# The cost figures of a list schedule: DMA transposes and overlapping VectorE operations (local attention beside a gated MLP, one core)

## The chip, the cores and the metric

The kernel runs on one core of a Trainium2 chip. The metric is the time of one execution on the device, in microseconds (us). The core has a matrix engine (PE, TensorE), a vector engine (DVE, VectorE), an activation engine (ACT, ScalarE), GpSimd (POOL) and a fifth one, SP (SyncE), which here does nothing but issue DMAs. Each engine takes its instructions strictly in the order in which they were written to its queue; engines wait for each other through semaphores.

## The reference

```python
x = A_x                                    # 1 x 2048 x 512, bf16
xn = layernorm(x)
# A: local, dilated attention: 32 heads of 16, window of 8 positions, dilation 2
q, k, v = split(xn @ wqkv)
logits[s, w] = q[s] . k[s - 2 w] * 0.25    # masked where s - 2 w < 0
o[s] = sum_w softmax(logits)[s, w] * v[s - 2 w]
A = o @ wo
# B: gMLP with a spatial gate, Fh = 896
z = gelu(xn @ w_in);  z1 = z[:, :896];  z2 = layernorm(z[:, 896:])
g = w_sp @ z2 + b_sp[:, None]              # w_sp is 2048 x 2048
B = (z1 * g) @ w_out
out = x + A + B
```

## The kernel before

The 2048 positions are cut into 16 blocks of 128 (index b) and 4 groups of 512 (index j or tc). The program is first written down as a list of some 900 tasks, each with an engine, an estimated duration (`est`), what it reads and writes, and a priority (a small number is urgent). `Plan.schedule` (L122) then plays the program through with these estimates and so fixes the order of every engine's queue; `Plan.emit` writes the queues and the semaphore waits. The estimates have no other effect: nothing of the planned times is in the program but the order.

The tasks, with the names used below:

- `ln_block(b)`, L569: x is loaded (`ldx`); DVE takes its statistics (`bnst` L574, `bnag` L576) and adds epsilon (`vpe` L597); POOL raises it to the power -0.5 (`rstd`, L600); DVE normalises (`norm`, L602); SP transposes the block by DMA (`xTd`, L606, 128 KB). The first four blocks are also centred (L582), transposed on PE (`xTr`, L589) and copied by ACT (L594), so that PE can start sooner. Warm-up matmuls (`warm`, L559) fill PE before that.
- `v_block` (L630 and on) makes v and stores it to DRAM (`Vw`, on POOL's queue, L638). `z2_block` (L728) makes the second half of z, with gelu and sums on ACT (L734, L739). `z2_wave(j)` works out its normalisation for four blocks at a time: four small DVE operations (L745 to L752), a power on POOL (`zr`, L755, estimate 1.9 us), four DVE normalisations (`zn`, L758).
- `qk_pair` (L647) makes q and k; `prods(j)` multiplies q with the eight shifted copies of k on DVE (`prod`, L668) and adds up four groups (`padd`, L673); PE reduces over the head dimension (`red`, L681, 32 small matmuls, priority 1); `softmax(j)` follows on DVE and ACT (L691 to L717).
- `z1_group` (L772) makes the first half of z, priority 200 and up.
- `ld_wT(tc)` transposes w_sp by DMA from DRAM (L829, 16 pieces of 512 KB, priority 6 and up). `g_group` (L856) multiplies with it, priority 300 and up; ACT copies the result (L864), DVE adds the bias and multiplies with z1 (`gb` L867, `u` L870).
- `pv_block(b)`: SP loads the eight shifted copies of v (`ldVs`, L879, 1 MB, priority 5); DVE multiplies with the attention weights and adds up (`pv` L884, L887, L890); SP transposes the result by DMA (`OTd`, L893, 128 KB, priority 2).
- `out_block(b)`: the residual is loaded (`ldxr`, L902, priority 4); PE multiplies OT with wo (L912) and the gated z1 with w_out (L921), priority 250 plus b (400 plus b for the last four blocks); DVE adds the residual (`fin`, L927); SP stores (`st`, L932, priority 3).

The schedule works as follows. For each engine it takes the candidate tasks whose dependencies are all planned, finds the earliest time at which one of them could start, and of all that could start within `tol` of this takes the one with the smallest priority. Of the engines' picks the earliest is planned. A compute task holds its engine for `est`. A task that depends on it is ready at its end plus a `hop`: 220 ns behind PE, 25 ns behind the same engine, 60 ns behind another, 100 ns behind a DMA. A DMA holds its queue for `issue` (480 ns on SP and ACT, 600 ns on POOL); 400 ns later it joins one line in which all transfers follow one another, at `dma_bw` bytes per ns, or `xbar_bw` for a transpose (265 at most in the first 7 us); it has landed 1300 ns after its turn ends. The estimate of a DVE operation of two tensors is c_tt(n) = 152 + n / 1.92 ns, so 2285 ns for 4096 elements; of bn_stats it is 685 ns.

Of the kernel before, what the change touches and what calls it, by code (L numbers as in the profile page):

```python
# [36 lines left out]
class Plan:  # L37
# [81 lines left out]
        return t  # L119


    def schedule(self, dma_bw=340.0, xbar_bw=190.0, dma_lat=1300.0, dma_pre=400.0, issue=None, tol=40.0):  # L122
        issue = issue or {"sp": 480.0, "act": 480.0, "pool": 600.0}
        for t in self.tasks:
            t.nwait = len(t.deps) + len(t.odeps)
            t.ready = 0.0
        for t in self.tasks:
            for d in t.deps | t.odeps:
                d.outs.append(t)
        cand = {e: [t for t in self.tasks if t.eng == e and t.nwait == 0] for e in ENGS}  # L130
        free = {e: 800.0 for e in ENGS}
        free["pool"] = 500.0
        free["sp"] = 790.0
        order = {e: [] for e in ENGS}
        dma_free = 0.0
        tbl = None
        slots = [dict(prev=None, avail=0.0) for _ in range(8)]
        left = len(self.tasks)

        def hop(d, t):  # L140
            if d in t.odeps:
                return 0.0
            if d.dma is not None:
                return 100.0
            if d.eng == "pe":
                return 220.0
            return 25.0 if d.eng == t.eng else 60.0

        def place(b, now):
            best = None  # L150
            if b.n == 2:
                opts = [(i, i + 1) for i in (0, 2, 4, 6)]
            else:
                opts = [(i,) for i in range(8)]
            for o in opts:
                if any(slots[i]["prev"] is not None and slots[i]["prev"].left > 0 for i in o):
                    continue
                av = max(slots[i]["avail"] for i in o)
                mate = 0.0
                if b.n == 1:  # L160
                    m = slots[o[0] ^ 1]
                    mate = 0.0 if (m["prev"] is not None and m["prev"].left > 0) else 1.0
                key = (max(av, now) + 300.0 * mate, av)
                if best is None or key < best[0]:
                    best = (key, o, av)
            return best

        while left:
            pick = None
            for e in ENGS:  # L170
                sc = []
                for t in cand[e]:
                    r = max(t.ready, free[e])
                    for b in t.banks:
                        if b.base is None:
                            p = place(b, r)
                            if p is None:
                                r = None
                                break
                            r = max(r, p[2])  # L180
                    if r is not None:
                        sc.append((r, t))
                if not sc:
                    continue
                st = min(r for r, _ in sc)
                near = [(t.prio, t.idx, r, t) for r, t in sc if r <= st + tol]
                near.sort(key=lambda x: x[:2])
                r, t = near[0][2], near[0][3]
                if e == "act" and t.tbl is not None and tbl is not None and t.tbl != tbl:
                    stay = [x for x in near if x[3].tbl in (None, tbl)]  # L190
                    if stay and stay[0][0] < t.prio + t.late:
                        r, t = stay[0][2], stay[0][3]
                if pick is None or r < pick[0]:
                    pick = (r, e, t)
            if pick is None:
                print("free", free, "slots", [(s_["prev"].name, s_["prev"].left) if s_["prev"] else None for s_ in slots])
                for e in ENGS:
                    print(e, [(t.name, t.ready, [(b.name, b.base) for b in t.banks]) for t in cand[e]][:12])
                raise RuntimeError("scheduler stuck")
            r, e, t = pick  # L200
            if t.drop and r > 9000.0:
                t.start = t.end = t.eng_end = r
                for b in t.banks:
                    b.left -= 1
                    if b.left == 0:
                        for sl in slots:
                            if sl["prev"] is b:
                                sl["avail"] = r
                cand[e].remove(t)
                left -= 1  # L210
                for o in t.outs:
                    o.ready = max(o.ready, r)
                    o.nwait -= 1
                    if o.nwait == 0:
                        cand[o.eng].append(o)
                continue
            for b in t.banks:
                if b.base is None:
                    _, o, av = place(b, max(t.ready, free[e]))
                    b.base = o[0]  # L220
                    prevs = {id(slots[i]["prev"]): slots[i]["prev"] for i in o if slots[i]["prev"] is not None}
                    for pb in prevs.values():
                        for u in pb.users:
                            if u.eng == e == "pe":
                                t.odeps.add(u)
                            elif u is not t:
                                t.deps.add(u)
                    for i in o:
                        slots[i]["prev"] = b
            t.start = r  # L230
            if t.dma is not None:
                iss = issue[e]
                t.eng_end = r + iss
                bw = xbar_bw if t.dma.get("xbar") else dma_bw
                xs = max(r + iss + dma_pre, dma_free)
                xe = xs + t.dma["nbytes"] / (bw if xs > 7000.0 else min(bw, 265.0))
                dma_free = xe
                t.end = xe + dma_lat
            else:
                dur = t.est  # L240
                if t.tbl is not None:
                    if tbl is not None and t.tbl != tbl:
                        dur += 1300.0
                    tbl = t.tbl
                t.eng_end = t.end = r + dur
            free[e] = t.eng_end
            for b in t.banks:
                b.left -= 1
                if b.left == 0:
                    av = max(u.end + (220.0 if u.eng == "pe" else 60.0) for u in b.users)  # L250
                    for s in slots:
                        if s["prev"] is b:
                            s["avail"] = av
            cand[e].remove(t)
            order[e].append(t)
            left -= 1
            for o in t.outs:
                o.ready = max(o.ready, t.eng_end if t in o.odeps else t.end + hop(t, o))
                o.nwait -= 1
                if o.nwait == 0:  # L260
                    cand[o.eng].append(o)
        self.order = order
        self.makespan = max(t.end for t in self.tasks)
# [736 lines left out]
```

## Time and profile before

| | |
|---|---|
| median of three runs | 241.48 us (241.38 to 242.04) |
| the profiled execution | 242.56 us |
| its span, first to last instruction | 240.0 us |
| granted PE clock, mean | 0.998 of full speed |
| PE busy | 233.5 us |
| DVE busy, instructions | 214.8 us, 271 |
| ACT, POOL busy | 98.3 us, 29.4 us |
| DMA transposes, SP | 16 (L606), 16 (L829), 16 (L893) |

The profile is one execution, recorded by the hardware. A row of a timeline gives the start in us, the duration in us, engine, line, operation, the tile written and the tile read, and the number of like instructions merged; in square brackets stands for how long the engine sat idle ahead of it and which instruction ended that. PE's matmuls overlap, so their durations are longer than their distance; the distance between starts is what counts. The times of a DMA on SP's queue are those of the issuing instruction; its landing is told separately. In the chain of waits "issue" is time in which an engine waited for nothing that the profile shows.

### The profile page before, as it was taken

What the parts mean: (1) busy time and instruction counts of PE and PEld (TensorE: products, weight loads), DVE (VectorE), ACT (ScalarE), POOL (GpSimd) and SP (SyncE); (2) the same over time, 40 slices, a digit from 0 to 9 for tenths busy, and PEclk for the clock granted to TensorE, in tenths of its full rate; (3) what the DMA queues carried; (4) which work ended last, traced back from release to release, by engine and by line L of the source; (5) the groups of instructions that cost most, each with busy time, mean ns of one, the idle gap of its engine ahead of it and who ended that gap; (6) DMA issues with size and microseconds to landing.
All of it is one profiled execution on the core that took longest, in us unless ns stands there. A gap on an engine that the chain in (4) does not pass through costs nothing.

```text
span 240.0 us, 3184 instructions
## 1 busy us (share of the span) xinstructions
PE 233.5 (97%) x1210; PEld 112.6 (47%) x1232; DVE 214.8 (90%) x271; ACT 98.3 (41%) x147; POOL 29.4 (12%) x56
## 2 busy tenths in 40 slices
PE   7999999999999999999999999999999999999994
PEld 4555555555444444544454444444444444444443
DVE  4868999898999999999999989989989999999932
ACT  2599869888898885721112111001010100101200
POOL 2566510406224100000000000000000000000000
PEclk9999999999999999999999999999999999999999
DMA  6997969999527210013079999999999978941121
GB/s 199 363 284 118 244 134 175 181 193 216 160 94 262 83 35 9 0 41 136 0 249 299 210 220 257 182 248 319 349 344 347 278 249 261 267 64 22 22 66 46
DMA packets 79966, 43.35 MB, mean 181 GB/s; under 512 B 52288, under 2 KB 79312, under 8 KB 79952
## 3 DMA queue, kind: packets, MB, share of 16 engines
q1 hardware_dynamic: 78720, 40.72, 67.1%
q0 software_dynamic: 800, 2.11, 2.4%
q10 hardware_dynamic: 432, 0.31, 0.4%
q8 instruction: 10, 0.16, 0.3%
q14 instruction: 4, 0.03, 0.1%
HBM read 26.35 MB, written 4.21 MB: 127 GB/s over the span
## 4 chain that ended last, share of the span: by engine, by line
PE 70%; DVE 19%; POOL 5%; ACT 3%; issue 1%; DVEq 0%; ACTq 0%
PE ps L856 40%; PE ps L921 10%; PE ps L772 10%; PE ps L912 6%; DVE arena L673 6%; DVE arena L668 6%; POOL fpool L755 3%; PE ps L559 2%; DVE arena L758 2%; POOL fpool L600 2%; ACT arena L734 2%; DVE arena L602 1%; PE ps L681 1%; DVE fpool L574 1%; PE ps L630 1%
## 5 line engine op out<-in xcount | busy, mean ns | idle before, releaser
L856 PE MATMUL ps<-arena 128*128 128x512 bf16 x437 | 98.2, 379 | 0.6
L856 PEld LDWEIGHTS ps<-arena 128*128 128x128 bf16 x448 | 43.7, 98 | 52.4
L864 ACT ACTIVATE arena<-ps 128x1024 bf16<-128x1024 f32 (+1 forms) x16 | 14.7, 917 | 103.8 <-PE ps L856 99.7
L668 DVE TENSOR_TENSOR arena<-arena 128x4096 bf16<-128x4096 bf16 x16 | 36.5, 2286 | 0.1
L884 DVE TENSOR_TENSOR arena<-arena 128x4096 bf16<-128x4096 bf16 x16 | 36.5, 2284 | 0.0
L887 DVE TENSOR_TENSOR arena<-arena 128x2048 bf16<-128x2048 bf16 (+1 forms) x32 | 30.5, 955 | 0.6
L647 PE MATMUL ps<-arena 128*128 128x512 bf16 x124 | 28.7, 379 | 0.2
L673 DVE TENSOR_TENSOR arena<-arena 128x4096 bf16<-128x4096 bf16 x12 | 27.5, 2291 | 0.3
L921 PE MATMUL ps<-arena 128*128 128x512 bf16 (+2 forms) x117 | 26.9, 366 | 0.1
L728 PE MATMUL ps<-arena 128*128 128x448 bf16 x128 | 26.0, 352 | 0.0
L772 PE MATMUL ps<-arena 128*128 128x512 bf16 x110 | 24.4, 379 | 0.1
L647 PEld LDWEIGHTS ps<-arena 128*128 128x128 bf16 x128 | 14.5, 113 | 13.0
L656 ACT ACTIVATE arena<-ps 128x1024 bf16<-128x1024 f32 x16 | 16.2, 1018 | 4.4 <-PE ps L647 3.2
L728 PEld LDWEIGHTS ps<-arena 128*128 128x128 bf16 x128 | 12.4, 98 | 11.7
L927 DVE TENSOR_TENSOR arena<-ps,arena 128x512 bf16<-128x512 f32 (+2 forms) x17 | 11.1, 656 | 7.5 <-PE ps L921 7.1
L921 PEld LDWEIGHTS ps<-arena 128*128 128x128 bf16 x119 | 11.5, 98 | 12.7
L772 PEld LDWEIGHTS ps<-arena 128*128 128x128 bf16 x112 | 10.8, 97 | 13.2 <-issue 0.4
L912 PE MATMUL ps<-arena 128*128 128x512 bf16 (+2 forms) x68 | 16.6, 366 | 0.0
L778 ACT ACTIVATE arena<-ps 128x1024 bf16<-128x1024 f32 (+1 forms) x16 | 14.0, 920 | 5.4 <-PE ps L772 5.3
L630 PE MATMUL ps<-arena 128*128 128x512 bf16 x61 | 15.9, 386 | 0.2
L739 ACT ACTIVATE arena<-arena 128x896 bf16<-128x896 bf16 x16 | 15.2, 949 | 0.1
L574 DVE BATCH_NORM_STATS2 fpool<-arena 128x6 f32<-128x512 bf16 x16 | 11.0, 687 | 2.4 <-DMA arena<-in_A_x_dram 2.4
(60 smaller groups left out, 178.0 us busy)
## 6 DMA issues: line engine op xcount, KB each, us to landing
arena<-vscr SPq DMA_DIRECT2D x16, 1024.0 KB, 6.2
arena<-in_A_x_dram SPq DMA_DIRECT2D x30, 128.0 KB, 4.0
vscr<-arena POOLq DMA_DIRECT2D x16, 128.0 KB, 2.8
out_dram<-arena SPq DMA_DIRECT2D x15, 128.0 KB, 4.2
arena<-in_A_wqkv_dram SPq DMA_DIRECT2D x2, 512.0 KB, 6.5
arena<-in_B_w_in_dram SPq DMA_DIRECT2D x2, 448.0 KB, 5.9
arena<-in_B_w_in_dram SPq DMA_DIRECT2D x1, 896.0 KB, 6.6
arena<-in_B_w_out_dram SPq DMA_DIRECT2D x1, 896.0 KB, 5.4
```

The source lines that it names most:

```text
L630: last = t.matmul(P(bk, 512), xTv(b, dc), AC(off["wv"] + 512 * dc, [[1, 512]]), start=(dc == 0), stop=(dc == 3))
L647: last = t.matmul(P(bk, 512, 512 * which), AC(off["wqk"] + 2048 * which + 512 * dc + c, [[4, 128]]), AC(off["xnT"] + dc * S + 512 * j, [[1 ...
L656: T("act", lambda a: a.activation(AC(qo, [[ko - qo, 2], [1, 512]]), P(bk, 1024).rearrange("p (t n) -> p t n", t=2), ACTF.Copy, scale=0.5), ...
L668: T("dve", (lambda pbv, qb, kb: lambda v: v.tensor_tensor(pbv, qb, kb, ALU.mult))(pbv, qb, kb), reads=rd, writes=[("pb", s_)], est=c_tt(40 ...
L673: T("dve", (lambda av, bv: lambda v: v.tensor_tensor(av, av, bv, ALU.add))(av, bv), reads=[("pb", 1)], writes=[("pb", acc)], est=c_tt(4096 ...
L728: last = t.matmul(P(bk, 448, 512 * hf), xTv(b, dc), AC(off["w_in2"] + 896 * dc + 448 * hf, [[1, 448]]), start=(dc == 0), stop=(dc == 3))
L772: last = t.matmul(P(bk, 512, 512 * i), AC(off["w_in1"] + 896 * dc + 128 * fc, [[1, 128]]), AC(off["xnT"] + dc * S + 512 * j, [[1, 512]]), ...
L856: last = t.matmul(P(bk, 512, 512 * i), AC(off["z2"] + FH * sh + 128 * fc, [[1, 128]]), AC(off["wT%d" % r_] + sh * 512, [[1, 512]]), start= ...
L884: T("dve", lambda v: v.tensor_tensor(tv, tv, av, ALU.mult), reads=[("attn", b)], writes=[("Vs", sv)], est=c_tt(4096), name="pv%d" % b, pri ...
L887: T("dve", (lambda n: lambda v: v.tensor_tensor(A("Vs", n, 4096 * sv), A("Vs", n, 4096 * sv), A("Vs", n, 4096 * sv + n), ALU.add))(n), wri ...
L912: last = t.matmul(P(bk, cn), AC(off["OT"] + 512 * tb + 128 * cc, [[1, 128]]), AC(off["wo"] + 512 * cc + c0, [[1, cn]]), start=(cc == 0), s ...
L921: last = t.matmul(P(bk, cn), AC(off["z1T"] + fc * S + 128 * tb, [[1, 128]]), AC(off["w_out"] + 512 * fc + c0, [[1, cn]]), start=False, sto ...
```

## The change

The change touches `Plan.schedule` alone. Five figures of the game are different:

```diff
-    def schedule(self, dma_bw=340.0, xbar_bw=190.0, ...
+    def schedule(self, dma_bw=340.0, xbar_bw=500.0, ...
...
-            return 25.0 if d.eng == t.eng else 60.0
+            if d.eng == t.eng == "dve":
+                return 100.0
+            return 25.0 if d.eng == t.eng else (135.0 if d.eng == "dve" else 60.0)
...
-                near = [(t.prio, t.idx, r, t) for r, t in sc if r <= st + tol]
+                near = [(t.prio, t.idx, r, t) for r, t in sc if r <= st + (110.0 if e == "dve" else tol)]
...
                 iss = issue[e]
+                if t.dma.get("xbar"):
+                    iss = 1300.0 if t.dma["nbytes"] <= 131072 else 3400.0
...
-                dur = t.est
+                dur = t.est - (75.0 if e == "dve" else 0.0)
```

A DMA transpose holds its queue for 1300 ns (128 KB) or 3400 ns (512 KB) where it held it for 480, and moves at 500 bytes per ns where it moved at 190. A DVE operation holds DVE for 75 ns less; its result is ready for DVE 100 ns and for another engine 135 ns after that, where it was 25 and 60. On DVE a task may be preferred that starts up to 110 ns after the earliest candidate, where it was 40. The tasks, their instructions, their tiles and their data are the same; a PSUM bank is given to a task in the order of the plan, so the bank of a tile can differ.

More of the change, by code (lines that the diff above doesn't have):

```diff
@@ L119, in add, with schedule @@
         return t
-    def schedule(self, dma_bw=340.0, xbar_bw=190.0, dma_lat=1300.0, dma_pre=400.0, issue=None, tol=40.0):
+    def schedule(self, dma_bw=340.0, xbar_bw=500.0, dma_lat=1300.0, dma_pre=400.0, issue=None, tol=40.0):
         issue = issue or {"sp": 480.0, "act": 480.0, "pool": 600.0}
```

## The prediction

> **What bounds the kernel now.** I read the page's busy table first, then its slices, then the waits of each engine, then the timelines of PE, DVE, POOL and SP.
>
> ```profile
> PE 233.5 (97%) x1210; PEld 112.6 (47%) x1232; DVE 214.8 (90%) x271; ACT 98.3 (41%) x147; POOL 29.4 (12%) x56
> ...
> PE   7999999999999999999999999999999999999994
> ...
> DVE  4868999898999999999999989989989999999932
> ```
>
> PE is full from the second slice to the last but one, DVE nearly so. Busy PE is only modelled, so I counted its work. From the timeline of PE the first useful matmul (L589) starts at 5.07 us; the last of L921 ends, and releases the last DVE add, at about 236.57: 231.5 us. In the chain of waits the g matmuls run like this:
>
> ```profile
> 101.11 10.74 PE ps L856 x49
> 111.85 0.05 issue
> 111.90 10.74 PE ps L856 x49
> 122.64 0.05 issue
> ```
>
> From 101.11 to 124.37 lie 108 of them (six groups of 16 and three quarters of the seventh): 0.215 us each, its 0.05 us pauses included. The others by their own rows, those 108 included: 917 matmuls of 512 columns x 0.215 = 197.2; 128 of 448 columns x 0.189 (32 in 6.06 us from 32.44 to 38.50) = 24.2; 128 small ones of L681 x 0.0247 (0.79 us for 32) = 3.2; 16 of L589 x 0.055 = 0.9; the last, split block about 2.4. Sum 227.9. So PE wastes 231.5 - 227.9 = 3.6 us at most between its first and last useful matmul. Before it lie 5.07 us (x arrives, DVE normalises), behind it 3.4 us to the span's end (last add, last store). **No order of the same operations can win more than that 3.6 us**, and most of it is the start: nine warm-up matmuls after 5.07 (0.8 us) and gaps of the first blocks. The later waits are these, the first two from the timeline of PE, the rest the whole list of PE's waits:
>
> ```profile
> 51.32 0.95 PE L681 MATMUL ps<-arena 128*128 128x32 bf16 x32 [0.46 <-DVE arena L673]
> 75.97 0.97 PE L681 MATMUL ps<-arena 128*128 128x32 bf16 x32 [0.16 <-DVE arena L673]
> ...
> PE ps L559 <- DVE arena L515: 1.3, 1, 1.3
> PE ps L681 <- DVE arena L673: 0.6, 2, 0.5
> ```
>
> Behind the warm-up (L559) PE waits 0.62 us in the whole kernel, both times for the last sum of a product group (L673, tasks padd0_3 and padd1_3) ahead of a reduction (L681, red0, red1).
>
> **The change part by part.** No operation is added or removed; the costs with which the list is made change, so each engine's fixed order may change, and the chip waits wherever that order asks for something that isn't there.
>
> *Transposes on SP.* The list gave every transpose 0.48 us of SP; now 1.3 (128 KB) or 3.4 (512 KB). The trace, by the views of the three lines:
>
> ```profile
> L606 SPq DMA_TRANSPOSE arena<-arena x16: 1200/1265/2436, 7.8 to 34.7; - x16
> ...
> L829 SPq DMA_TRANSPOSE arena<-in_B_w_sp_dram x16: 1716/2392/7242, 36.0 to 153.9; - x16
> ...
> L893 SPq DMA_TRANSPOSE arena<-arena x16: 1191/1202/1280, 144.2 to 227.5; - x16
> ```
>
> (min/median/max ns). 1.3 is right; 3.4 is 1.0 over the median, but six of the big ones from 125.24 took 18.95 us, 3.16 each. With the bandwidth now 500, a small one lands in the plan 1.3 + 0.4 + 0.26 + 1.3 = 3.26 us after issue starts (before 0.48 + 0.4 + 0.69 + 1.3 = 2.87); measured medians are 4.1 (L606) and 3.5 (L893). SP will thus seldom be planned too early. What this can move is the place of OTd (priority 2), stores (3), residual loads (4), Vs loads (5) and weight transposes (6 and up) among each other from 124 us on: when SP is planned busy, several are ready at once and priority decides. Gain on PE's path: none to take, since PE never waits there. Cover: from SP's rows and the 3.5 us, OT landed some 2.3 us ahead of its first matmul (L912) for block 0, 3.1 for block 5, 1.4 for block 9, about 0 for block 10, 3.0 for block 15. While that lasts the cost is 0.
>
> *DVE's overlap.* An instruction now occupies DVE 0.075 us less; one that needs its result still waits 0.1 (DVE) or 0.135 (others). For a dependent one nothing changes (bnst: 685 + 25 = 610 + 100); an independent one comes 0.075 earlier. The timeline of DVE shows this to be right:
>
> ```profile
> 71.30 2.29 DVE L668 TENSOR_TENSOR arena<-arena 128x4096 bf16<-128x4096 bf16 x1
> 73.62 2.29 DVE L673 TENSOR_TENSOR arena<-arena 128x4096 bf16<-128x4096 bf16 x1
> 75.83 2.28 DVE L668 TENSOR_TENSOR arena<-arena 128x4096 bf16<-128x4096 bf16 x1
> ```
>
> 2.32 us to the sum that needs the product, 2.21 to the next, independent product. The Trainium skill speaks against it: "VectorE: DVE Perf Modes", section "The DRAIN you can't avoid", says the next operation doesn't start until the pipe is empty, though it points to exceptions. By that rule the new list would hold DVE 271 x 0.075 = 20.3 us too fast and the kernel would end far later; by the rows it loses nothing, and the measurement decides.
>
> What it does: up to 271 x 0.075 = 20.3 us of planned DVE time go (the bound, were all independent). That allowance was false per instruction, but it paid for things the list still counts too short, so DVE reached its joins with PE not much late. Slack of the sum against the reduction that needs it, from both timelines: red0 -0.46, red1 -0.16, red2 100.09 - 99.17 = +0.9, red3 124.21 - 122.85 = +1.4 us. Since red has priority 1, the list puts it on PE at the instant its sum is planned to be ready; a sum late on the chip holds up the PE queue behind it, g, z1 and V included.
>
> *What is still counted too short.* The pow on POOL (L755), estimate 1.9 us:
>
> ```profile
> 44.16 3.00 POOL L755 TENSOR_TENSOR fpool<-fpool 128x4 f32<-128x4 f32 x1 [13.26 <-DVE fpool L752]
> ...
> 56.88 3.00 POOL L755 TENSOR_TENSOR fpool<-fpool 128x4 f32<-128x4 f32 x1 [1.39 <-DVE fpool L752]
> ...
> 79.89 1.04 POOL L755 TENSOR_TENSOR fpool<-fpool 128x4 f32<-128x4 f32 x1 [1.96 <-DVE fpool L752]
> ```
>
> Beside a 2.28 us product it takes 3.0, beside L696 1.04. Twice DVE then sits 0.91 and 0.93 us (L758) on a sum's path. The list sees none of it: 0.9 late at red0, 1.8 by red1. A Vs load is planned 0.48 + 0.4 + 3.08 + 1.3 = 5.3 us and measured 6.2.
>
> *DVE's window of choice* grows from 40 to 110 ns: a more urgent task may be awaited up to 0.11 us. At most some tens of such choices, about half a microsecond of DVE per ten, in a stage where DVE had 2.2 us of idle time for rstd (L602 behind L600) that the new list sees and may fill with the next bn_stats. I take 0 for the end: neither reaches PE while the reds set it.
>
> *Sum for PE:* lower bound -0.62 (both waits go) less perhaps 0.6 of the start; upper bound +1.8 - 0.62 = +1.2 at the reds, plus 0.9 if Vs loads come late with no slack left. I take one late pow at its full price, +0.9, less the 0.62 that PE waits there already: **+0.3 us**. Only one, since the second wave may come to lie beside a shorter operation, as the last one did. The profiled execution took 242.56 us with a span of 240.0 (2.56 around it); span about 240.3, 242.9 profiled. The runs shown have a median of 241.48, 1.08 under the profiled one, so **241.8**.
>
> **Rivals.**
>
> *Both pow waits turn into PE waits* (slower). For: reds are placed with no slack; red0 and red1 have already waited. Against: 0.6 us of it is already paid, and products may now start earlier by the filled rstd waits. It decides once the sum is planned over 0.62 us ahead of what the chip does. Price +1.2 to +1.5: **242.8**.
>
> *The out blocks lose their lead* (slower). Priority 250 puts them before g as soon as OT is planned to land. Their measured lead, 0 to 3.9 us, shrinks; a Vs load 0.9 late holds pv, OTd, then PE; a late add holds the store on SP (L932 sat there up to 1.87 us) and with it the next OTd. 0.9 + 1.6 = +2.5: **244.0**. Against: transposes are now planned at their true queue time.
>
> *Fewer waits* (faster). The 0.62 goes and 0.3 to 0.6 of the first 12 us: -0.9: **240.6**. For: the costs come nearer to the rows. Against: little is there to win, and the start follows x, bn_stats, centring, transpose and copy, whose latencies are unchanged.
>
> *The order hardly changes:* 241.5, inside the forecast.
>
> **How the numbers follow.** A measurement can tell about 0.3%, 0.72 us. Within it 0.41 (forecast and unchanged order); slower 0.38 (reds 0.27, out blocks 0.11); faster 0.21. Point 241.8. The range takes in the faster case and both waits at full price, and cuts half of the out-block case: 240.4 to 243.5. Both signs hold much, so the likeliest case's own range: 241.0 to 242.2.
>
> **What would show it.** Right: PE's waits still name L681 behind L673, 0.5 to 1.5 us in sum, and PE 97% busy. First rival: over 1.5 us there. Second: waits of L912 for a transpose or for L879. Faster: no wait of L681 and a first L647 matmul before 17.12. I am wrong if the pow's row stays at 1.0 everywhere, if DVE waits for Vs loads, or if ACT, 41% busy, shows up as a releaser of PE.

## The result and the profile after

The changed kernel takes **257.27 us** (median of 6 runs, 255.32 to 257.87); the kernel before, run beside it, 241.79 us (241.38 to 242.78). The ratio is 1.062, 95% interval 1.058 to 1.067: slower by 15.5 us, where the prediction had 241.8 us and a range of 240.4 to 243.5. The profiled execution took 257.87 us with a span of 255.4 at a mean granted clock of 0.993.

The diff adds four lines ahead of the tasks, so every line of the kernel before stands 4 further down: `red` is L685, `padd` L677, `z1` L776, `z1g` on ACT L782, `Ve` (ACT's copy of v) L639, its store `Vw` L642, `zr` L759, `rstd` L604, `OTd` L897, the weight transposes L833, the first matmul of an out block L916. In the experiments two more lines can be added (L916 becomes L918).

The page's busy row of PE, its slices and the granted clock by slices:

```profile
PE 236.4 (93%) x1210; PEld 112.5 (44%) x1231; DVE 215.2 (84%) x271; ACT 101.5 (40%) x149; POOL 31.9 (12%) x56
...
PE   8999999799989499999999878697899999999995
...
PEclk9999999999999979999999999999999999999999
```

The work is the same; PE now has holes: one "4" in slice 14 (83 to 89 us), shallower ones between slices 23 (140 us) and 29, and a clock of "7" in slice 15, behind the deepest hole. Smaller dips in slices 8 and 12 (45 to 51 and 70 to 77 us) are two reductions. The waits of PE say what the holes are (sum in us, number of times, longest):

```profile
PE ps L916 <- DMA arena<-arena: 7.9, 7, 2.0
PE ps L776 <- ACT arena L782: 3.8, 1, 3.8
PE ps L685 <- DVE arena L677: 1.4, 1, 1.4
...
PE ps L685 <- ACT arena L639: 0.8, 1, 0.8
```

Seven times an out block stood at the head of PE's queue before its OT had landed; once z1 waited for a PSUM bank that ACT empties; two reds waited. With the 0.2 us of z1 that the list puts down to issue this is 14.1 us behind the warm-up, against 0.62 before: 13.5 more. The rest is in the timeline of PE:

```profile
88.23 1.84 PE L776 MATMUL ps<-arena 128*128 128x512 bf16 x6 [3.75 <-ACT arena L782]
90.29 12.76 PE L776 MATMUL ps<-arena 128*128 128x512 bf16 x52 [0.22 <-issue]
...
143.68 1.04 PE L916 MATMUL ps<-arena 128*128 128x512 bf16 x4 [1.06 <-DMA arena<-arena]
...
165.05 1.04 PE L916 MATMUL ps<-arena 128*128 128x512 bf16 x4 [2.00 <-DMA arena<-arena]
```

From 88.23 to red2 at 102.88 the 60 or so z1 matmuls take 0.244 us each and not 0.215: the granted clock is 0.62 from 88.3 to 92 us and 0.92 to 96, 0.38 x 3.7 + 0.08 x 4 = 1.7 us lost. A third term comes from how a wait is counted: from the modelled end of the matmul ahead, 0.379 us after its start, where PE would have started the next one after 0.215. So each wait costs 0.16 us more than its row says; there are ten waits against two, 1.3 us more. 13.5 + 1.7 + 1.3 = 16.5; PE's last matmul ends 16.2 us later than before, and the stretch behind it is 0.8 us shorter. So the loss is PE waiting, and being slow behind one wait. The first out block now stands at 143.68 in PE's queue; before it came at 150.04, 3.3 us after its OT had landed.

The cause of the out blocks' waits is in the timeline of SP:

```profile
141.09 1.27 SPq L897 DMA_TRANSPOSE arena<-arena  x1
142.41 0.58 SPq L883 DMA_DIRECT2D arena<-vscr  x1
143.09 4.64 SPq L833 DMA_TRANSPOSE arena<-in_B_w_sp_dram  x1
147.77 1.27 SPq L897 DMA_TRANSPOSE arena<-arena  x1
```

and the same of the kernel before:

```profile
145.54 0.58 SPq L879 DMA_DIRECT2D arena<-vscr  x1
146.17 4.68 SPq L829 DMA_TRANSPOSE arena<-in_B_w_sp_dram  x1
150.90 1.26 SPq L893 DMA_TRANSPOSE arena<-arena  x1
```

A weight transpose behind one load of Vs holds SP for 4.6 us, in both. Before, six of them had gone ahead of OT0 and only two stood between OTs; now four do (4.64, 4.45, 4.59, 5.24 us). Each is planned at 3.4, so SP falls behind by 1.24 + 1.05 + 1.19 + 1.84 = 5.3 us over four blocks, and the four out blocks after the first wait 1.41 + 0.81 + 2.00 + 1.23 = 5.5.

That the kernel before had a lead to spare lies in its plan, the times by which `Plan.schedule` makes the order (they follow from the program; no trace shows them). There OT0 is issued at 140.3 us and lands at 150.7, 10.5 us later, because six weight transposes at 190 bytes per ns stand ahead of it in the one line of transfers; OT1 to OT3 get 13.2, 11.4 and 9.8 us. On the chip these four took 2.5, 4.1, 2.5 and 5.1 us from issue to landing. The queue was booked too cheaply (OT0 was issued at 144.2), the transfer far too dearly, and the second error covered the first. At 500 bytes per ns the line is empty: the plan of the changed kernel gives each of them 3.3 us. The chip takes 2.5 to 3.3, so this figure is right, and nothing is left to cover SP's late issues. No run separates the bandwidth from the queue time.

### The profile page after: what moved, and what is told of

The parts are those of the page before. It is cut to its first block, busy times and chain, and to the rows that moved or that the text cites. A ratio compares the mean times of both kernels' runs of the same rounds, so it can differ in the third digit from the quotient of the medians.

```text
span 255.4 us, 3185 instructions
## 1 busy us (share of the span) xinstructions
PE 236.4 (93%) x1210; PEld 112.5 (44%) x1231; DVE 215.2 (84%) x271; ACT 101.5 (40%) x149; POOL 31.9 (12%) x56
## 4 chain that ended last, share of the span: by engine, by line
PE 40%; DVE 35%; DMA 11%; POOL 6%; ACT 4%; issue 4%; DVEq 0%; ACTq 0%
PE ps L860 17%; DVE arena L672 9%; PE ps L925 8%; DMA arena<-arena 7%; PE ps L776 6%; DVE arena L677 5%; PE ps L916 5%; DMA vscr<-arena 4%; DVE arena L891 3%; DVE arena L888 2%; POOL fpool L759 2%; POOL fpool L604 2%; PE ps L563 2%; DVE fpool L578 1%; DVE arena L700 1%
## 5 line engine op out<-in xcount | busy, mean ns | idle before, releaser
L860 PE MATMUL ps<-arena 128*128 128x512 bf16 x437 | 98.6, 379 | 0.6
L776 PE MATMUL ps<-arena 128*128 128x512 bf16 x109 | 26.0, 395 | 4.1 <-ACT arena L782 3.8
L651 PE MATMUL ps<-arena 128*128 128x512 bf16 x125 | 28.6, 379 | 0.2
L677 DVE TENSOR_TENSOR arena<-arena 128x4096 bf16<-128x4096 bf16 x12 | 27.5, 2289 | 0.3
L916 PE MATMUL ps<-arena 128*128 128x512 bf16 (+2 forms) x68 | 16.7, 368 | 7.9 <-DMA arena<-arena 7.9
L776 PEld LDWEIGHTS ps<-arena 128*128 128x128 bf16 x112 | 11.2, 101 | 18.3 <-ACT arena L782 4.5
L871 DVE TENSOR_TENSOR arena<-arena 128x1024 bf16<-128x1024 bf16 (+1 forms) x16 | 9.9, 618 | 9.1 <-ACT arena L868 9.0
L782 ACT ACTIVATE arena<-ps 128x1024 bf16<-128x1024 f32 (+1 forms) x16 | 14.0, 917 | 7.0 <-PE ps L776 7.0
L634 PE MATMUL ps<-arena 128*128 128x512 bf16 x61 | 15.7, 387 | 0.2
```

The source lines that it names most:

```text
L634: last = t.matmul(P(bk, 512), xTv(b, dc), AC(off["wv"] + 512 * dc, [[1, 512]]), start=(dc == 0), stop=(dc == 3))
L651: last = t.matmul(P(bk, 512, 512 * which), AC(off["wqk"] + 2048 * which + 512 * dc + c, [[4, 128]]), AC(off["xnT"] + dc * S + 512 * j, [[1 ...
L677: T("dve", (lambda av, bv: lambda v: v.tensor_tensor(av, av, bv, ALU.add))(av, bv), reads=[("pb", 1)], writes=[("pb", acc)], est=c_tt(4096 ...
L776: last = t.matmul(P(bk, 512, 512 * i), AC(off["w_in1"] + 896 * dc + 128 * fc, [[1, 128]]), AC(off["xnT"] + dc * S + 512 * j, [[1, 512]]), ...
L860: last = t.matmul(P(bk, 512, 512 * i), AC(off["z2"] + FH * sh + 128 * fc, [[1, 128]]), AC(off["wT%d" % r_] + sh * 512, [[1, 512]]), start= ...
L916: last = t.matmul(P(bk, cn), AC(off["OT"] + 512 * tb + 128 * cc, [[1, 128]]), AC(off["wo"] + 512 * cc + c0, [[1, cn]]), start=(cc == 0), s ...
```

## The experiments

All runs stand beside runs of the kernel before on the same chip; ratios are to those. "Waits" are PE's, behind the warm-up.

**Each half alone.** e1 is the changed kernel with the old figures of the transposes (190 bytes per ns, 480 ns of queue); e2 is the kernel before with the new ones only.

```diff
 e2, on the kernel before
-    def schedule(self, dma_bw=340.0, xbar_bw=190.0, ...
+    def schedule(self, dma_bw=340.0, xbar_bw=500.0, ...
+                if t.dma.get("xbar"):
+                    iss = 1300.0 if t.dma["nbytes"] <= 131072 else 3400.0
```

> The changed kernel with the DMA transposes counted as in the kernel before (0.48 us of SP, 190 bytes per ns); only the VectorE figures are new. Theory (the lost allowance on VectorE takes the lead from PE's joins): this half carries the loss, PE waits again at the reductions, at z1 and at the out blocks, 253 to 258 us. Rival (the queue time of the transposes reorders SP and carries the loss): 241 to 243 us.

> The kernel before with the DMA transposes counted at 1.3 and 3.4 us of SP and 500 bytes per ns; VectorE as before. Theory: VectorE's allowance still hides what is counted too short, PE keeps its lead, 241 to 243 us, waits of PE under 2 us in sum. Rival (the SP figures carry the loss): 250 us or more, with PE waits for the transposes of the attention result.

e1: 246.39 us, ratio 1.020 (1.017 to 1.023). No out block waits (OT keeps its lead; in this plan it again lands 11 to 13 us after its issue for the first four blocks), the reds wait 4.2 us. e2: 249.06 us, 1.031 (1.027 to 1.034). The reds wait 0.2; the list of waits:

```profile
PE ps L914 <- DMA arena<-arena: 5.5, 3, 3.8
```

Behind the 3.80 us one the clock is 0.50 for 5.1 us. Neither expectation held: both halves cost, by different waits: the VectorE figures through the reds, the queue figures through the out blocks. They don't add up exactly (4.7 + 7.4 against 15.5), since every plan is another order.

**The out blocks.** e6 leaves the changed kernel's order alone and makes the last four weight transposes small; e3 tells the planner that OT lands 3 us later; e10 rearranges SP by hand; e8 gives the planner SP times near the measured ones; e9 gives it a large lead at both places.

```diff
 e6
+                nb_ = 1 if tc == 3 else NB      # destination and source cut to nb_ * 128 columns
 e3, in hop
-                return 100.0
+                return 3100.0 if d.name.startswith("OTd") else 100.0
 e10, on the finished order
+        put("sp", ["ldVs2", "ldVs3"], "OTd0")
+        for i_ in range(4):
+            put("sp", ["wT3_%d" % i_], "ldVs%d" % (4 + i_))
 e8
-                    iss = 1300.0 if t.dma["nbytes"] <= 131072 else 3400.0
+                    iss = 1300.0 if t.dma["nbytes"] <= 131072 else 2300.0 + 2500.0 * nvs   # Vs loads since the last big one
 e9, in hop
+            if t.name.startswith("red"):
+                return 2600.0
-                return 100.0
+                return 8100.0 if d.name.startswith("OTd") else 100.0
```

(`put` moves the named tasks ahead of another in one engine's order; e8 also books `zr` at 3.0 us.)

> The changed kernel, all orders the same, but the last four weight transposes on SP move one block of 128 columns instead of 16 (the rest of that quarter of the weights is left out). Theory S (the out blocks wait because SP sits 4.5 to 5.2 us at each weight transpose that stands behind a Vs load and ahead of a transpose of the attention result): the 7.9 us of PE waits for those transposes fall under 1.5 us, 247 to 251 us. Theory L (PE, VectorE and SP hold each other up in a loop, or the out blocks simply stand too early): 5 us or more of the waits stay, 253 to 257 us.

> The changed kernel, but the plan holds a landed transpose of the attention result ready for PE 3 us later, so that the out blocks stand some 2.6 us further back in PE's queue. Theory L (a loop: PE late, so the add late, so SP and the next transpose late): the 7.9 us of waits go to under 1 us, 249 to 251 us. Theory S (SP's own queue runs late, 4.6 us instead of 3.4 for each weight transpose, whatever PE does): the lateness of 6 to 8 us stays and 3 us of it is covered, 4 to 5 us of waits stay, 253.5 to 255.5 us.

> The changed kernel, all orders the same but SP's: the third and fourth Vs load stand behind the first four weight transposes instead of ahead of them, and each of the last four weight transposes stands ahead of the Vs load that it stood behind. Nothing is left out. Theory S (a weight transpose is slow on SP because of the Vs load ahead of it): each of the five takes 2 to 3 us instead of 4.5 to 7.5, and the 7.9 us of PE waits for the attention transposes fall under 2 us, 248 to 251.5 us. Rival (its length depends on the traffic at that time, whatever the order): it stays at 4 us or more, and so do the waits, 254 to 257 us.

> The changed kernel with the figures that its own traces show: a weight transpose holds SP 2.3 us and 2.5 us more for each Vs load issued since the last one, the power takes 3.0 us. Theory (a list whose costs are right has no waits on PE, but a greedy one pays for it in an order that leaves PE without work): waits for transposes under 2 us where the list puts an out block early, but SP serves results first and the weights late, 245 to 249 us. Rival (right figures are all that is missing): 241 us or less.

> The changed kernel with all its figures, but for PE the plan holds a reduction's input ready 2.5 us later and a transposed attention result 8 us later than it computes, so that these tasks stand further back in PE's queue. Theory (the loss is the lost lead of PE's joins and nothing else): all waits of PE behind the warm-up fall under 1.5 us in sum, 241 to 243.5 us. Rival (the work itself comes later by the new order of VectorE and SP): the waits move to other joins or to the end, 246 us or more.

e6: 248.82 us, 1.030 (1.027 to 1.034): 8.4 us less than the changed kernel by the duration of four transfers alone. Its waits:

```profile
PE ps L776 <- ACT arena L782: 3.8, 1, 3.8
PE ps L685 <- DVE arena L677: 1.7, 1, 1.7
...
PE ps L918 <- DMA arena<-arena: 0.5, 1, 0.5
```

7.9 us at the out blocks have become 0.5; z1 waits as before, red0 0.4 us more, and 0.7 us is new at two early joins. Some 1.7 of the 8.4 us is clock: behind z1's wait it stayed at 1.00 in this execution. e3: 253.55, 1.049 (1.042 to 1.057), with still 5.5 us there, as Theory S had it: a margin of 3 us bought 2.4, because the lateness grows with each block, so that a fixed lead is used up. The rest of e3's gain is at z1, see below. e10: 252.65, 1.044 (1.037 to 1.050), between the two expectations, out waits 3.9: by its SP rows the four weight transposes ahead of OT0 take 1.9 to 3.2 us (in the changed order the first of them, behind three Vs loads, takes 7.5), and the four put ahead of their Vs loads 3.1 to 4.9, not the 2 to 3 that Theory S had; and OT0 then stood behind two more loads, and the first block waited 2.58. e8: 254.22, 1.053 (1.036 to 1.069): the out blocks' waits fall to 2.0, but weights now come late (one wait of 3.6 us for w_sp at 215 us, clock 0.50 behind it), so a truer cost isn't enough by itself. e9: 251.61, 1.042 (1.035 to 1.049): no red and no OT wait at all, and in their place 4.1 us where v's matmul waits for ACT and 1.7 at each of two joins with DVE. The out waits follow the time that the plan allows from the issue of an early OT to its first matmul: 7.9 us of waits at 3.3 us (the changed kernel), 5.5 at 6.3 (e3), none at 11 and more (e9 and e1).

**The wait at z1.** In the changed kernel the chain of waits runs from a power on POOL over a store of v into ACT and so to PE (start, duration, what):

```profile
71.00 3.01 POOL fpool L759
...
75.21 5.57 DMA vscr<-arena
...
80.87 0.60 ACT arena L639
...
88.23 1.84 PE ps L776 x6
```

ACT's copy of v for block 15 (`Ve15`) reuses a buffer that a store must have left. It sat 3.48 us for that, with a softmax exponential, two z2 sums and the emptying of z1's banks behind it. The store is the third of four on POOL behind the power, issued at 75.21 us, 0.2 us after the load of w_out on SP. e4 puts ACT's next steps ahead of Ve15; e14 moves the loads that start on SP at 75.01 (w_out 896 KB, then wo) behind the first Vs load, so to 107 us; e15 is e9 with e14's edit.

```diff
 e4
+        put("act", ["z2s14", "z2s15", "sexp1", "Ve15"], "z1g0_0")
 e14
+        put("sp", ["ldVs1"], "ldwout")
```

> The changed kernel with four neighbours in ACT's queue in another order: the two squares and the exponential go ahead of the copy of the last v block, which waits 3.5 us for a store. Theory Z (PE's 3.8 us wait in z1 and the slower matmuls behind it come from ACT sitting at that copy): the wait shrinks by about 3 us and the matmuls run at 0.215 us again, 251 to 253 us. Rival (the stage behind is set by SP and VectorE in any case): the z1 wait goes, but PE waits as much longer for the transposes, 256 us or more.

> The changed kernel with one edit in SP's order: the loads of w_out (ldwout) and of wo (ldwo0 to ldwo3) stand behind ldVs1, so that they go at some 109 us and not at 75. Nothing else is moved and nothing left out. Theory C (the store of v lands late because the load of w_out is issued within some 1 us of it): ACT's wait for the store's landing (L639 <- DMA vscr<-arena, 3.5 us in the changed kernel) falls under 1 us, PE's wait at z1 (L776 <- ACT, 3.8) under 0.8, the matmuls behind it take 0.215 us again and not 0.247; the out blocks' waits stay (6 to 9 us). Time 251 to 254 us against 257.3. Rival N (the store is slow by itself, or by the step on POOL that stands in its midst): the wait at z1 stays at 3 to 4 us and the time at 255 to 258.

> The edit of e9_lead (the planner keeps 2.5 us before each red and 8 us behind each OT block) and the late loads of w_out together. Theory C with the lead theory: neither red nor out block waits, and the 4.1 us that the V step waited for ACT in e9_lead go as well: no PE wait over 1.8 us behind the warm-up, 245 to 247.5 us. Rival N: a wait of 3 us or more at V or z1 stays, 250 us or more. In both cases a rest of some 3 us over the kernel before is left for the weights of the last steps, which the planner still books too cheaply.

e4: 253.17 us, 1.048 (1.045 to 1.051): the z1 wait is 0.2, the clock undisturbed; 7.1 us at the out blocks stay. e14: the store lands in time (ACT's Ve wait at most 0.27 us each, for PE), although the power still stands in the midst of the stores (71.42 us, 3.01). By itself this doesn't show that the loads made it late, since in e10, whose orders differ from the changed kernel's on SP alone and only from 120 us on, the z1 wait is 0.55 with the loads in place (0.50 in e3). The stores and the load of the changed kernel, and of e10:

```profile
73.98 2.31 POOL L642 DMA_DIRECT2D vscr<-arena  x4
75.01 0.38 SPq L838 DMA_DIRECT2D arena<-in_B_w_out_dram  x1
...
74.61 2.31 POOL L642 DMA_DIRECT2D vscr<-arena  x4
76.33 0.38 SPq L838 DMA_DIRECT2D arena<-in_B_w_out_dram  x1
```

In e10 PE waits 0.9 us longer at red0, the load comes later, and the third store is issued 0.5 us ahead of it: it lands in 2.1 us. Over all traces that keep the load at its place the line is sharp: a store issued 0.32 us or more ahead of the load of w_out landed in 1.9 to 2.1 us, one issued from then until 0.75 us behind it in 3.3 to 5.8. So the load made the store late, not POOL. POOL and SP race here, and the same order can have the wait or not. But the time of e14 is 261.64 us, 1.083 (1.080 to 1.086), against 251 to 254 expected. Its PE timeline:

```profile
86.15 13.12 PE L776 MATMUL ps<-arena 128*128 128x512 bf16 x58 [0.56 <-ACT arena L782]
...
148.29 1.87 PE L916 MATMUL ps<-arena 128*128 128x512 bf16 x4 [8.19 <-DMA arena<-arena]
```

The wait of 3.8 at z1 has gone and one of 8.2 has come at the first out block: PE is there 2.5 us sooner, and the moved loads now stand between the first Vs load and the other three, so that the first weighted sum waits 5.2 us for its Vs and OT0 is issued at 144.5 and not 141.1. Behind it the clock is 0.50. I had moved a transfer into the one stretch in which SP's queue decides. e15: 253.04 us, 1.046 (1.040 to 1.052), not 245 to 247.5. V's wait fell from 4.1 to 1.0 as theory C said, but PE then waited 3.9 us for an add of an out block (L862 <- DVE L933, clock 0.50 behind it), and 1.5 more at a second: DVE, busy with the weighted sums, came to that add late. Another 2.2 us came at q and k behind red0. On the cause of the late store both runs agree with theory C; as repairs both failed.

**The reds.** e7 takes the second norm's power away; e11 moves the masks and the first stores on POOL behind the powers of the first norm; e13 lets PE do one group more before red0 and red1 in the kernel before; e16 puts DVE's window back to 40 ns and leaves the rest of the change.

```diff
 e7
-  g.tensor_tensor(..., ALU.pow)                    # zr
+  g.memset(Fv("rstd2", 4, 4*j), 1.0)
 e11
+        put("pool", ["mask2", "mask3", "Vw0", "mask4", "mask5", "mask6", "mask7"], "zr0")
 e13, on the kernel before
+        put("pe", ["z2_12_1"], "red0_0")
+        put("pe", ["z1_1_0"], "red1_0")
 e16
-                near = [... if r <= st + (110.0 if e == "dve" else tol)]
+                near = [... if r <= st + tol]
```

> The changed kernel, all orders the same, but the four powers on GpSimd for the second normalisation are left out: a constant is written instead. Theory R (the power takes 3.0 us beside a product where the list says 1.9, so the sums and the stores of v behind it are late): the waits of PE at the reductions fall from 2.2 us to under 1, and the idle 0.9 us of VectorE ahead of the normalisations goes; the waits for the transposes stay at 7 to 8 us; 251 to 254 us. Rival (the reductions come too early for VectorE's own pace): the waits at the reductions stay over 1.5 us, 254 to 257 us.

> The changed kernel, all orders the same but GpSimd's: six small memsets and the store of the first v block stand behind the powers of blocks 9 to 11 instead of between them. Theory P (the store waits for the landing of an earlier one on its channel, holds the powers behind it, and so VectorE and the first sum): VectorE's wait of 1.1 to 1.9 us at the normalisation of block 9 goes, and PE's wait at the first reduction falls from 1.4 us to under 0.5; the later waits stay; 1 to 1.5 us less than the changed kernel, 254 to 256.5 us, or 251 to 253.5 if the wait in z1 is short. Rival (the list counts VectorE itself too fast): the wait at the first reduction stays over 1 us.

> The kernel before with two exchanges on PE: the first and the second reduction each stand one group of four matmuls further back (0.8 us), so that their sums are there. If each wait of PE is a loss at the end, as the theory has it, the 0.62 us go: 241.0 to 241.3 us, a ratio of 0.997 to 0.998. If the waits were covered by something later, no change within 0.1%.

> The changed kernel with one figure put back: the planner's window for VectorE and GpSimd is the old one again (40 ns), the queue's figures and the shorter VectorE bookings stay, and it plans anew. If the wider window is what took the lead from the red steps and moved GpSimd's steps, the red waits (1.4 and 0.8) fall to about 0.6 together and the time to 250 to 254. If the shorter bookings of VectorE did it, the time stays at 254 to 258 with waits at red and at z1. Either way the out blocks wait 5 to 8 us, since the queue's figures are kept.

e7: 252.91 us, 1.047 (1.044 to 1.050), the time that Theory R gave, but by another path: without the power the stores go out ahead of the load of w_out, and z1 waits 0.5. Red0 still waits 1.70: the power that I had priced isn't what holds red0. e11: 256.75, 1.061 (1.054 to 1.068): the red waits on DVE are gone, which points to POOL's order as the cause of red0's. In the changed order the store Vw0 stands ahead of a power:

```profile
20.73 0.61 POOL L642 DMA_DIRECT2D vscr<-arena  x1 [1.11 <-DMA vscr<-arena]
21.36 0.57 POOL L604 TENSOR_TENSOR fpool<-fpool 128x1 f32<-128x1 f32 x1
...
24.02 2.53 POOL L604 TENSOR_TENSOR fpool<-fpool 128x1 f32<-128x1 f32 x1 [1.09 <-DVE fpool L601]
```

It waits 1.11 us for an earlier store to land, DVE's normalisation behind it 1.14, and a later power of that kind takes 2.53 us beside a product that now comes early (0.55 elsewhere). Runs that have this order bear it out: in e4 the store waits for no landing and red0 waits 0.1; in e10 it waits 2.28 and red0 2.21. But the time doesn't move: the out blocks wait 8.4 instead of 7.9. e13: 0.998 (0.996 to 1.001), no difference that can be told; the reds' waits are gone, and 0.4 us at an out block and 0.3 at z1 have come. e16: 251.17 us, 1.038 (1.033 to 1.043; a third run, 253.90 us, isn't in the ratio), 6 us under the changed kernel: z1 waits 0.5, the reds 0.4 and 1.9, the out blocks 5.3, and the clock stays at 1.00. That the window took 6 of the 15.5 us is not shown: 3.3 of them are z1's wait, which e3 and e10 lack with the wide window too, and 1.7 are the clock behind it. The 2.6 us at the out blocks are what remains for the new order, in one execution. (The expectation names GpSimd's window too; the edit is VectorE's alone.) The reds' waits did not go as I had expected, so the shorter bookings hold a share of them.

**All at once.** e12 joins the orders of e4, e10 and e11. e17 joins those of e4 and e11 with e6's small transposes; e18 cuts the four ahead of OT0 as well.

> The changed kernel with three queues in another order at once: SP as in e10, ACT as in e4, GpSimd as in e11. If the loss is the sum of these three late queues, PE's waits behind the warm-up fall to 1 to 3 us in sum and the time to 242 to 245 us. If PE only finds other joins late instead, 247 us or more.

> Three edits of the changed kernel at once, so that every wait found so far but the first out block's is taken away: ACT's order of e4_act_order, GpSimd's order of e11_pool, and the last four weight transposes cut to a sixteenth as in e6_small_wT3 (that work is left out, so the last quarter of the gate's product isn't the reference's). If a wait that goes is only passed on to the next step that TensorE shares with the queue (theory J), the some 6 us that TensorE gains before 140 us go into the first out block, whose OT0 still stands on SP behind four full weight transposes and three loads of Vs (141.1 us): L916 waits some 5 us there, and the time stays at 246 to 249 (e6 had 248.8). If waits add up one by one (theory A), the 3.8 us at z1, its 1.9 us of slow matmuls and the red waits come off e6's time: 242 to 243.5.

> The kernel of e17_act_wT3 with the four weight transposes ahead of OT0 cut to a sixteenth too (left out: half of the gate's product). Theory J: OT0 is now held by VectorE's first products of the weighted sum alone (137.0 us in the changed kernel), so that the first out block waits 1 to 3 us and not some 5; 1.5 to 4 us under e17's time, 243 to 246. Theory A: no more than 1 us under e17's time. If both come out at 247 or more, there is a wait that none of the runs has shown.

e12: 249.82 us, 1.032 (1.026 to 1.039), 3.5 us of out waits left, the first 2.21 with a clock of 0.50 behind it for 3.4 us. e17: 244.9 us, 1.016 (1.011 to 1.020); e18: 244.56 us, 1.014 (1.011 to 1.016). All the waits of e17 behind the warm-up:

```profile
PE ps L685 <- DVE arena L677: 2.0, 2, 1.3
...
PE ps L685 <- ACT arena L639: 0.8, 1, 0.8
PE ps L651 <- DMA arena<-arena: 0.7, 1, 0.7
PE ps L634 <- ACT arena L598: 0.2, 1, 0.2
PE ps L918 <- DMA arena<-arena: 0.2, 1, 0.2
PE ps L776 <- ACT arena L782: 0.2, 1, 0.2
```

4.1 us against 0.62 before: 3.5, and the time is 244.9 - 241.4 = 3.5 above the kernel before. The account closes within a microsecond. Theory J, that the gain is passed on to the first out block, fails here: SP comes forward with the rest (OT0 issued at 135.3 us, not 141.1), and e18 wins no more than 0.3 us. Theory A said 242 to 243.5 for e17; the rest above that is at other reds: red2 waits 1.31 us and red3 0.65, which had slack as long as PE stood at z1. Waits are passed on in e11 and e14, and add up in e17; which of the two depends on whether the late queue itself moves.

No version found is measurably faster than the kernel before.

## Why the prediction was wrong

1. *"PE is the bound, and no order can win more than 3.6 us"*: right, and the frame was right: every microsecond of the loss is a wait of PE or a slow clock behind one. It said nothing on how much an order can lose.

2. *"SP will thus seldom be planned too early … While that lasts the cost is 0"*: **this step failed**, worth 7.4 us of waits by e6. I had an OT land 3.26 us after its issue in the new plan against 2.87 in the old, and so took the new figures for the more careful ones. That sum leaves out the line: behind the weight transposes the old plan allowed 9.8 to 13.2 us for the first four blocks, so the change took 6 us and more of lead away. I compared 3.4 us with the median row (2.39) and took it for safe, though I had the row that refutes it: the transposes right behind Vs loads, 7.24 of "min/median/max" and the two at 146 and 154 us, 4.7 each. The cost depends on what stands ahead, and the ones behind a Vs load are those between the OTs. And I took the lead as given ("cover: 2.3 us for block 0"; row by row it was 3.3 there, and 0.5 to 2.4 for the next eleven) while the change was free to use it up.

3. *Rival 2, out blocks lose their lead, 244.0, chance 0.11*: the right mechanism at the right place, with the wrong price. I charged one late Vs and one late store, 2.5 us; lateness is added at each block, 1.1 to 1.8 us four times, and the wait of PE behind it is paid each time: 7.9 in all, with the first block and two later ones. "Against: transposes are now planned at their true queue time" was the error of step 2 over again.

4. *"+0.9 for one late power, less 0.62" at the reds*: wrong in cause and short in size. The reds wait 2.2 us in sum and not 0.9 (0.8 of it for ACT), and by e7 the power `zr` isn't behind red0; by e11 it is POOL's new order in the first 25 us. I had read POOL's row for its durations only, not for what a store ahead of a power does. That power's 2.53 us beside a product does repeat what `zr`'s rows showed.

5. *"ACT, 41% busy, shows up as a releaser of PE" as a sign that I am wrong*: it did, with 3.8 us at z1 and 0.8 at a red. The path (a load on SP slows a store of POOL's, that holds ACT, that holds PE's PSUM) crosses four queues, none of them busy; I had costed each engine's row, not the buffers between them. e4 removes it by ACT's order; a store 0.5 us ahead of the load removes it too (e10).

6. *The clock*: not in my sum at all. A wait of PE has a second price, here 1.7 us, in e2 0.50 x 5.1 = 2.6.

7. *DVE's window, "I take 0 for the end"*: not 0. e16 is 6 us faster, though of this only the 2.6 at the out blocks can't come from the race at z1 and the clock behind it. The window hardly costs DVE anything; it changes what else is ready, and so the order of the other queues.

8. *DVE's overlap of 75 ns*: right as a row; busy DVE is 215.2 us, as before (214.8). Truer figures made a worse order: the old ones, too long on DVE and far too slow in the line of transfers, held a reserve ahead of the joins. For DVE this is argued, from e1's 4.2 us at the reds.

The Trainium skill has a rule on point 6. "TensorE: Matmul & The Clock Gate", section "HAM oscillation — how this bites in real kernels", advises no idle gap of PE beyond some 3.4 us. The rows here agree only in part: the clock fell to 0.50 behind waits as short as 1.69 (e8), 1.78 (e14) and 2.21 (e10, e12), and behind 3.75 (the changed kernel), 3.80 (e2) and all over 3.84; it stayed at 1.00 behind 2.76 (e3), 3.26 (e16) and 3.84 (e6). The same page's Part 1 says that the window runs freely, which would let the phase decide; no run here shows the phase.

On point 4, the Trainium skill's page "SBUF — State Buffer", section "SBUF: two separate sides", says that VectorE and GpSimd lock a shared port pair for a whole instruction. The rows agree: 2.53 and 3.0 us for powers beside a 2.28 us product, 0.55 and 1.0 elsewhere; that it is this lock isn't shown by a run.

What stays open: why the changed kernel's runs spread over 255.3 to 257.9 us. The race between the store and the load of w_out would do it: without the z1 wait, and with the longer red waits of e10, I estimate from the rows 257.9 - 3.4 + 1.0 = 255.5; but only one execution is recorded. How much the wider window, the shorter bookings and each of the two transpose figures hold by themselves stays open too.

## What to carry to other kernels

When a planner's costs change, ask first of every join what lead it has, and whether the new costs let the plan spend it; a bound engine with 0.6 us of waits has all to lose. Take a transfer's cost from the rows at the place that matters, by what stands ahead of it, not from the median, and multiply a shortfall by the number of blocks that repeat it. A fixed margin mends a cost that is too short at each step only when it is as large as the shortfalls together (3 us wasn't, 8 was), and its price can turn up elsewhere. When one figure is put right, look for the error that it had covered. Moving one transfer to cure one wait can make a larger one where its new queue decides.

## What the runs showed of the hardware

- From 125 us on, a 512 KB DMA transpose holds SP in the changed kernel for 2.1 to 3.0 us behind another, 4.5 to 5.2 behind one 1 MB Vs load, 7.5 behind three (over all runs 1.9 to 3.6, 3.1 to 6.0, 4.3 to 8.7). It lets SP go at about the time when what stands ahead lands: the four between the OTs end at 147.7, 155.3, 161.9 and 171.4 us, the Vs loads ahead of them land at 148.0, 154.8, 162.1 and 171.6. Cut to a sixteenth, behind a Vs load, it took 1.1 to 1.7 (e6, e17): both its own size and what is ahead count.
- A 128 KB store on POOL's queue landed in 1.9 to 2.1 us when it was issued 0.32 us or more ahead of an 896 KB load on SP, and in 3.3 to 5.8 when it was issued less than that ahead, or up to 0.75 us behind. In e14, without the load, the median is 2.0 (66 to 90 us).
- Behind a wait of PE the granted clock can halve, for 3.4 us or a multiple (6.8 in e2, 10.2 in e14). The length of the wait alone doesn't decide: it halved behind 1.69 us (e8) and stayed at 1.00 behind 3.84 (e6).
